# A long-convolution and feed-forward kernel: six of eight product groups copied whole out of PSUM, GpSimd's time counted in full by the planner, and one PSUM buffer for two quarters of the inverse

## The chip, the cores and the metric

The kernel runs on one core of one Trainium2 chip. The metric is the device time of one execution in microseconds (us). Before the change the median of three runs is 644.57 us, from 643.6 to 645.45. One further execution was profiled: it took 642.35 us, of which 640.6 us lie between its first and last instruction (its span).

In the profile the engines are PE (matmuls), PEld (PE's weight loads, which overlap the matmuls), DVE (VectorE), ACT (ScalarE), POOL (GpSimd) and SP (SyncE, which here issues transfers).

## The reference

Two branches work on 2048 positions of 640 channels, and a gate per position mixes them.

```python
def _A_ref(u, log_A_real, A_imag, C_real, C_imag, log_dt, D_skip):
    ...
    P = jnp.exp((A * dt[:, None])[:, :, None] * pos[None, None, :])
    K = 2.0 * jnp.einsum("dn,dnl->dl", C, P).real
    ...
    y = jnp.fft.irfft(Uf * Kf[None, :, :], L2)[:, :, :L]
    return y + u * D_skip[None, None, :]

def _B_ref(x, w1, w2):
    h = jnp.maximum(jnp.einsum("bsd,df->bsf", x, w1), 0)
    return jnp.einsum("bsf,fd->bsd", h, w2)

g = _sigmoid((x * gate_w).sum(-1, keepdims=True))
return g * a + (1 - g) * b
```

Branch A builds one filter of 2048 taps for each channel from 128 complex modes and convolves the channel with it. Branch B is a two-layer network with 1728 hidden units. All arithmetic is in 32 bits.

## The kernel before

**The feed-forward branch** runs in three parts over the hidden units (`PARTS`), each over eight groups of 256 positions. Every matrix is split in a high and a low half, so that a product takes three matmuls. Its matmuls write the PSUM tile `pf` (two banks in turn); ACT and DVE take the hidden layer out of it (`hh`, `hl`), and DVE merges the sums of the second layer into `q`. These are the fillers: most have the lowest rank on PE.

**The generator** (up to about 404 us) makes the filter taps with sines and exponentials on ACT and multiplications on DVE, and POOL adds the skip term to a tile `kt`.

**The convolution** (`conv`, from about 404 us on) is a transform of 4096 points, done in five blocks of 128 channels (i = 0 to 4). One block goes through:

- *first step* (`stage1`): matmuls with a table `tf` on the filter (`ck`, `cl`) and on the input (`xu`), and DVE transposes into the large tile `ku`, which has two halves, K and U, for eight groups j;
- *second step* (`stage2`), for each group j: 32 small matmuls with the table `tm` write one PSUM buffer `pc`, whose two halves are the spectra of the filter and of the input. ACT copies the filter half to SBUF, over the group's K. DVE multiplies it by the imaginary part of the input, read from PSUM, into the group's U, and then by the real part, in place. POOL forms the complex product with a subtraction and an addition;
- *inverse of the second step* (`inv2`), for each half h of four groups: 128 matmuls with the table `tn` into two buffers `pc`, copied back by ACT;
- *relay*: eight DVE transposes from U to K;
- *last step* (`inv1`): for each j of two and each quarter q of two, matmuls with the table `tw` (two in the code, four rows in the profile) write one buffer `pc`, from which ACT takes four gated columns into `yo`. POOL joins parts of the feed-forward sum to these, and SP stores them.

The PSUM ring `psc` has three buffers `pc` of two banks each. All four steps take from it; `inv2` takes two at once. Another ring, `K`, has two tiles `ku`, so the next block's first step can run while this block is in its second.

**The order of all work** is written by a planner (`Plan`) before the program exists. Every piece of work is a task with an engine, an assumed duration, tasks it depends on, ring tokens that it takes and uses, and a rank (lower is sooner). `Plan.run` repeatedly picks the task that can start soonest and issues it; the engines then execute in exactly this order, each as a fixed queue, and wait where reality is later than the plan. A token goes back to its ring when its last user ends. A task with `port=True` lengthens DVE's assumed time when POOL is assumed busy; before the change only the generator's DVE tasks have this mark. On PE the plan prefers to stay with fillers (mode `f`) until two convolution tasks (`c`, `c1`) are ready or 3 us have passed, and it charges 0.2 us for a change of mode. SP's queue is part of the same order.

`stage2` puts its eight matmul tasks, then `inv2` for h = 0 and for h = 1, into one queue `s2`, so that they reach PE in this order. The multiplications have rank `S2D` = 1 on DVE, merges and hidden-layer corrections rank 0, relays rank 2.

Of the kernel before, what the change touches and what calls it, by code (L numbers as in the profile page):

```python
# [10 lines left out]
F32 = mybir.dt.float32  # L11
# [14 lines left out]
S4R = 3  # L26
# [27 lines left out]
S2D = 1  # L54
# [5 lines left out]
PL = 2.5  # L60
YO = 5
YJ = 3
KRANK = 3
TN = 0.7

# [76 lines left out]
class Plan:  # L142
# [79 lines left out]
    def run(self):  # L222
        self.free = {e: 0.0 for e in self.LAG}
        mode, dma, log, done, block, since = {}, 0.0, [], 50.0, 0.0, 0.0
        heads = {k: 0 for k in self.queues}
        while True:
            best = None
            for e in self.LAG:
                c, soon = [], []
                for (eng, q), n in heads.items():  # L230
                    if eng == e and n < len(self.queues[eng, q]):
                        t = self.queues[eng, q][n]
                        r, known = self.ready(t)
                        for g in t.glue:
                            r2, k2 = self.ready(g)
                            r, known = max(r, r2), known and k2
                            for b in t.take:
                                k = sum(x.ring is b.ring for x in (*t.take, *g.take))
                                r = max(r, sorted(b.ring.slots)[k - 1] if len(b.ring.slots) >= k else 1e9)
                        (c if known else soon).append((r, t))  # L240
                if not c:
                    continue
                at = max(self.free[e], min(r for r, _ in c))
                key = lambda t: t.prio + (0.5 if t.mode is not None and mode.get(e) not in (None, t.mode) else 0)
                r, t = min((x for x in c if x[0] <= at), key=lambda x: key(x[1]))
                start = max(at, r)
                if e == 'PE' and mode.get(e) == 'f':


                    if t.mode in self.BURST and at - since < self.PATIENCE and self.burst(c, heads, at) < self.GATHER:  # L250
                        other = [x for x in c if x[1].mode == 'f' and x[0] <= at + .05]
                        if other:
                            r, t = min(other, key=lambda x: key(x[1]))
                            start = max(at, r)
                if e == 'PE' and (t.mode != 'f' or mode.get(e) != 'f'):

                    for r2, t2 in c:
                        if key(t2) < key(t) and r2 <= at + self.HOLD:
                            t, start = t2, max(at, r2)
                    hold = [r2 for r2, t2 in soon if t2.prio < t.prio and r2 <= at + self.HOLD]  # L260
                    if hold:
                        at = max(hold)
                if best is None or at < best[0]:
                    best = at, e, t, start
            if best is None:
                break
            _, e, t, start = best
            change = self.CHANGE.get(e, 0) if t.mode is not None and mode.get(e) not in (None, t.mode) else 0
            if e == 'PE' and t.mode != 'f':
                since = start + t.dur  # L270
            if t.mode is not None:
                mode[e] = t.mode
            for b in t.take:
                b.ring.slots.remove(min(b.ring.slots))
            t.fn()
            self.free[e] = start + change + t.dur
            if e == 'PE':

                done += t.n
                while done >= 128:  # L280
                    done -= 128
                    at = self.free[e] - t.dur * done / t.n
                    fetch = self.FETCH + (self.BUSY if dma > at + 2 else 0)
                    self.free[e] += max(0, block + fetch - at)
                    block = max(at, block + fetch)
            if t.port:

                self.free[e] += 0.25 * min(max(self.free['POOL'] - start, 0), t.dur)
            t.end = self.free[e] + t.lag
            if t.kb:  # L290
                dma = max(dma, start + min(t.dur, 0.62) + 0.5) + t.kb / (230 if start < 12 else 270)
                t.end = max(dma, start + t.dur) + 1.1
            for b in (*t.take, *t.use):
                b.left -= 1
                b.free = max(b.free, t.end)
                if b.left == 0:
                    b.ring.slots.append(b.free)
            heads[e, t.q] += 1
            log.append((start, t))
        stuck = [(k, self.queues[k][n]) for k, n in heads.items() if n < len(self.queues[k])]  # L300
        assert not stuck, [(k, len(self.queues[k]) - heads[k]) for k, _ in stuck]
        self.log = log
# [42 lines left out]
class Kernel:  # L345
# [865 lines left out]
    def conv(self, C=128):  # L1211
        tc, nc, io, A, tok, ring = self.tc, self.nc, self.io, self.plan.add, self.plan.token, self.plan.ring
        V, S, P, D_ = self.V, self.S, self.P, self.D
        n, H = D // C, C // 2
        od = self.out.rearrange("(a h b) d -> h a b d", h=2, b=16)
        ud = io['A_u'][0].rearrange("(a b) d -> a b d", b=32)
        for k, v in dict(psc=3, ck=2, ckp=2, cu=1, yo=YO, yj=YJ, K=2).items():
            ring(k, v)
        st = {}

# [96 lines left out]
        def stage2(i, j, dep):  # L1317
            b_ = tok('psc')

            def pe():  # L1320
                ps = self.psc.tile([128, 2, 4, C], F32, name="pc")
                for a in range(2):
                    for m in range(4):
                        for p in range(2):
                            r, g = slice(p * 64, p * 64 + 64), 4 * j + m
                            x = st['ku', i].rearrange("p j k (e m t) -> p j m k e t", m=4, t=2)
                            self.E.matmul(ps[32 * m:32 * m + 32, p, 2 * a:2 * a + 2].rearrange("q k (e t) -> q k e t", t=2),
                                          st['tm'][r, g, 32 * a:32 * a + 32], x[r, j, m], start=True, stop=True)
                st['p2', i, j] = ps.rearrange("q p (a k) c -> q k a p c", a=2)

            def copy():
                S.copy(whole(i, j), st['p2', i, j][:, 0])

            def mul(a):
                def go():
                    k = whole(i, j)
                    V.tensor_mul(whole(i, j, 'U') if a else k, st['p2', i, j][:, 1, None, a].to_broadcast([128, 2, 2, C]), k)
                return go

            def add(k):  # L1340
                def go():
                    y, x = whole(i, j)[:, k], whole(i, j, 'U')[:, 1 - k]
                    (P.tensor_add if k else P.tensor_sub)(y, y, x)
                return go
            f = A('PE', None, 0.92, pe, dep, take=[b_], use=[K[i]], rank=S2P, mode='c', n=32)
            c = [A('ACT', 's2', 0.52, copy, [f], use=[b_, K[i]], rank=0.5)]
            for a in (1, 0):
                c.append(A('DVE', 's2', 0.62, mul(a), c, use=[b_, K[i]], rank=S2D))
            return f, [A('POOL', 's2', 0.7, add(k), c, use=[K[i]], rank=1) for k in range(2)]


        def whole(i, j, k='K'):
            return st[k, i][:, j].rearrange("q (b p c) -> q b p c", b=2, p=2)
# [40 lines left out]
        def inv1(i, j, dep):  # L1394
            last = i == n - 1
            for q in range(2):
                b_, b0 = tok('psc'), j * 8 + q * 4
                ns = min(max(2 * sum(c <= i for c in CG) - b0, 0), 4)
                y_ = tok('yo') if ns or not last else None
                g_, first = None, False  # L1400
# [1 line left out]
                    first = self.gy_tok is None  # L1402
                    g_ = self.gy_tok = self.gy_tok or tok('K')

                def pe(q=q, b0=b0):
                    py = st['p4', i, b0] = self.psc.tile([128, 2, 4, C], F32, name="pc")
                    for h in range(2):
                        self.E.matmul(py[h * 64:h * 64 + 64, 0].rearrange("p b c -> p (b c)"), st['tw'],
                                      st['K', i][:, h * 4 + b0 // 4], start=True, stop=True)

                def copy(q=q, b0=b0, ns=ns, y_=y_, first=first):
                    if first:
                        self.gy = self.pr.tile([128, 8, 2, 512], F32, name="ku", bufs=2).rearrange("p j k (b c) -> p (j k b) c", c=C)
                    if y_:
                        st['yo', i, b0] = self.pr.tile([128, 4, C], F32, name="yo", bufs=YO)
                    x = st['p4', i, b0][:, 0].rearrange("p b c -> p (b c)").rearrange("p (c b) -> p b c", b=4)
                    for b in range(4):
                        o = self.gy[:, b0 + b] if last and b >= ns else st['yo', i, b0][:, b]
                        S.mul(o, x[:, b], self.gate[:, b0 + b:b0 + b + 1])
                a = A('PE', 's4', 0.87, pe, [*dep, tw], take=[b_], use=[K[i]], rank=S4R, mode='c1')  # L1420
                pes['4', i, b0] = a
                if JS4 and q:
                    self.plan.join([pes['4', i, b0 - 4], a])
# [117 lines left out]
```

## Time and profile before

| | |
|---|---|
| median of three runs | 644.57 us (643.6 to 645.45) |
| profiled execution | 642.35 us, span 640.6 us |
| granted PE clock | 1.00 over the whole span |
| transfers | 107.78 MB, mean 168 GB/s |
| ACT busy from 404 to 641 us | 82 us of 237 |
| POOL busy from 404 to 641 us | 83 us of 237 |

In the profile's rows a group of instructions is named by the tile it writes and the tiles it reads, `out<-in`; nearly all carry line 314, the helper that pins each instruction in the planner's order. "Idle before" is time in which the engine did nothing ahead of the group, with what ended that wait. In the view by stretches each row is a stretch of the span with the busy time and number of instructions of each engine. In the view in order of time, rows of the same kind that follow each other are merged, with their count.

### The profile page before, as it was taken

The page shows a single profiled execution, that of the slowest core. Times are in us where ns is not written, and L with a number is a line of the kernel's source. Part 1 is how long each engine was busy: PE and PEld are TensorE (multiplying, and loading weights), DVE is VectorE, ACT ScalarE, POOL GpSimd, SP SyncE. Part 2 cuts the span into 40 slices and gives each one's busy share as a digit, 9 for nine tenths or more (in the row PEclk, how much of TensorE's full clock was granted, in tenths as well). Part 3 has the DMA queues.
Part 4 walks back from the last instruction along what each step waited for, and adds up shares of the span by engine and source line. Part 5 has one row for each costly group of instructions (what it writes and reads, how often), then busy time and mean ns, then how long its engine had stood idle before and what let it go on. Part 6 is the DMA issues. An engine that isn't in the chain of part 4 may idle for free.

```text
span 640.6 us, 19212 instructions
## 1 busy us (share of the span) xinstructions
PE 617.3 (96%) x8236; PEld 503.0 (79%) x8236; DVE 508.5 (79%) x818; ACT 402.1 (63%) x603; POOL 93.9 (15%) x134
## 2 busy tenths in 40 slices
PE   7989999899999899999999999999999999999897
PEld 6989998798898798898898898665565556756577
DVE  4889936989999999998999999768579753966542
ACT  5557439999999988988978985113443424432550
POOL 0000000000000000000000000024151531713633
PEclk9999999999999999999999999999999999999999
DMA  9974774333456734373454225794406558156355
GB/s 256 326 236 147 221 229 165 105 125 112 136 167 210 255 122 144 122 242 117 129 198 154 79 80 176 258 315 132 144 3 215 185 164 263 53 158 188 102 166 133
DMA packets 76176, 107.78 MB, mean 168 GB/s; under 512 B 7610, under 2 KB 58682, under 8 KB 75195
## 3 DMA queue, kind: packets, MB, share of 16 engines
q1 hardware_dynamic: 75930, 106.14, 53.2%
q8 instruction: 65, 1.06, 0.7%
q10 hardware_dynamic: 160, 0.41, 0.3%
q14 instruction: 21, 0.16, 0.1%
HBM read 67.47 MB, written 44.30 MB: 174 GB/s over the span
## 4 chain that ended last, share of the span: by engine, by line
PE 56%; DVE 5%; DMA 2%; ACT 2%; issue 1%; SPq 1%; DVEq 0%; ACTq 0%
PE pf L314 35%; PE pc L314 13%; PE pk L314 4%; DVE ku L314 3%; PE pg L314 2%; PE px L314 2%; DMA part<-q 1%; ACT ku L314 1%; PE pe L314 1%; DMA out_dram<-yo 1%; SPq L314 1%; DVE sn L314 1%; ACT cs L314 0%; DVE q L314 0%; ACT q L314 0%
## 5 line engine op out<-in xcount | busy, mean ns | idle before, releaser
L314 PE MATMUL pf<-xx,w1h 128*128 128x256 f32 (+1 forms) x760 | 184.2, 339 | 0.4 <-DVE xx L314 0.3
L314 PEld LDWEIGHTS pf<-xx,w1h 128*128 128x128 f32 x760 | 125.2, 189 | 22.8 <-issue 7.3
L314 PE MATMUL pf<-xx,w1l 128*128 128x512 f32 (+1 forms) x340 | 115.7, 340 | 0.0
L314 PE MATMUL pf<-w2h,hh 128*128 128x320 f32 x288 | 89.7, 315 | 2.4 <-DVE hl L314 1.5
L314 PE MATMUL pf<-w2l,hh 128*128 128x320 f32 x288 | 87.8, 309 | 0.0
L314 ACT COPY ku<-pc 128x512 f32<-128x512 f32 (+1 forms) x60 | 43.8, 761 | 68.2 <-PE pc L314 56.7
L314 PE MATMUL pf<-w2h,hl 128*128 128x320 f32 x256 | 73.3, 312 | 0.0
L314 PEld LDWEIGHTS pf<-xx,w1l 128*128 128x128 f32 x340 | 64.3, 189 | 7.6 <-DVE w1l L314 0.2
L314 POOL TENSOR_TENSOR kt<-kt,dsk 128x8 f32<-128x8 f32 x20 | 10.3, 515 | 392.7 <-DVE kt L314 377.8
L314 POOL TENSOR_TENSOR ku<-ku 128x256 f32<-128x256 f32 x80 | 56.2, 737 | 55.3 <-DVE ku L314 49.1
L314 DVE TENSOR_TENSOR ku<-pc,ku 128x512 f32<-128x512 f32 x80 | 52.6, 684 | 12.5 <-ACT ku L314 11.3
L314 DVE STREAM_TRANSPOSE ku<-pc 128x512 f32<-128x512 f32 x80 | 50.2, 683 | 13.7 <-PE pc L314 13.7
L314 PEld LDWEIGHTS pf<-w2h,hh 128*128 128x128 f32 x288 | 54.1, 188 | 7.7 <-issue 3.7
L314 DVE TENSOR_TENSOR sn<-pg,cs 128x1024 f32<-128x1024 f32 x40 | 48.7, 1217 | 7.5 <-ACT cs L314 7.5
L314 PEld LDWEIGHTS pf<-w2l,hh 128*128 128x128 f32 x288 | 54.1, 188 | 0.6
L314 ACT ACT_TABLE_LOAD x42 | 53.9, 1283 | 0.7
L314 ACT CAST cs<-pg 128x1024 int32<-128x1024 f32 x40 | 40.3, 1008 | 21.2 <-PE pg L314 21.0
L314 DVE TENSOR_TENSOR mg<-mg,cs 128x1024 f32<-128x1024 f32 x40 | 48.9, 1222 | 1.3
L314 PEld LDWEIGHTS pf<-w2h,hl 128*128 128x128 f32 x256 | 46.4, 188 | 3.5 <-issue 2.9
L314 PE MATMUL pc<-ku,tm 64*32 64x256 f32 x1280 | 42.2, 392 | 3.6 <-DVE ku L314 2.4
L314 ACT ACTIVATE cs<-cs,half_pi 128x1024 f32<-128x1024 f32 x40 | 45.6, 1140 | 0.0
L314 ACT ACTIVATE hh<-pf 128x512 fp32r<-128x512 f32 (+1 forms) x40 | 20.5, 513 | 39.4 <-PE pf L314 39.4
(170 smaller groups left out, 1232.5 us busy)
## 6 DMA issues: line engine op xcount, KB each, us to landing
xx<-xt SPq DMA_DIRECT2D x24, 640.0 KB, 6.8
xt<-xx SPq DMA_DIRECT2D x16, 640.0 KB, 3.9
part<-q SPq DMA_DIRECT2D x16, 640.0 KB, 3.4
q<-part SPq DMA_DIRECT2D x16, 640.0 KB, 5.3
ws<-in_B_w_dram SPq DMA_DIRECT2D x20, 320.0 KB, 5.5
kd<-kt SPq DMA_DIRECT2D x80, 64.0 KB, 1.8
ub<-in_A_u_dram SPq DMA_DIRECT2D x10, 512.0 KB, 4.7
xu<-ub SPq DMA_DIRECT2D x5, 1024.0 KB, 6.2
```

What stands on the lines that cost most here:

```text
L314: self._last = self._tc.keep_in_program_order(f(*a, **k))
```

## The change

In `stage2`, for the groups j = 0, 1, 2, 4, 5 and 6 of every block (`FULL`), ACT copies all 1024 columns of the buffer into the group's K and U (before: 512 columns into K). Both multiplications of DVE then read the input's spectrum from U in SBUF in place of PSUM, and the first writes a new SBUF tile `ut` of a ring of two in place of U. They no longer use the PSUM token, so the buffer is free after the copy. POOL's two additions read `ut` and give it back. Groups 3 and 7 stay as they were. The plan's duration of the copy is 0.96 in place of 0.52 for full groups, and their multiplications are marked `port`.

In `Plan.run` the share of POOL's remaining time that is charged to a `port` task goes from a quarter to the whole.

In `inv1` the two quarters of one j write the two halves of one buffer `pc`: the second quarter takes no token of its own, and the buffer is free when both are copied.

```diff
+FULL = (0, 1, 2, 4, 5, 6)
+UT = 2
+FULLR = 0
...
-                self.free[e] += 0.25 * min(max(self.free['POOL'] - start, 0), t.dur)
+                self.free[e] += 1.0 * min(max(self.free['POOL'] - start, 0), t.dur)
...
-        for k, v in dict(psc=3, ck=2, ckp=2, cu=1, yo=YO, yj=YJ, K=2).items():
+        for k, v in dict(psc=3, ck=2, ckp=2, cu=1, yo=YO, yj=YJ, K=2, ut=UT).items():
...
+            full = j in FULL
+            t_ = tok('ut') if full else None
+
             def copy():
-                S.copy(whole(i, j), st['p2', i, j][:, 0])
+                if full:
+                    S.copy(st['ku', i][:, j].rearrange("q k (a p c) -> q k a p c", a=2, p=2), st['p2', i, j])
+                else:
+                    S.copy(whole(i, j), st['p2', i, j][:, 0])
...
                     k = whole(i, j)
-                    V.tensor_mul(whole(i, j, 'U') if a else k, st['p2', i, j][:, 1, None, a].to_broadcast([128, 2, 2, C]), k)
+                    u = whole(i, j, 'U')[:, a] if full else st['p2', i, j][:, 1, a]
+                    if a:
+                        st['x2', i, j] = whole(i, j, 'U')
+                        if full:
+                            st['x2', i, j] = self.pr.tile([128, 4 * C], F32, name="ut", bufs=UT).rearrange("q (b p c) -> q b p c", b=2, p=2)
+                    V.tensor_mul(st['x2', i, j] if a else k, u[:, None].to_broadcast([128, 2, 2, C]), k)
...
-                    y, x = whole(i, j)[:, k], whole(i, j, 'U')[:, 1 - k]
+                    y, x = whole(i, j)[:, k], st['x2', i, j][:, 1 - k]
...
-            c = [A('ACT', 's2', 0.52, copy, [f], use=[b_, K[i]], rank=0.5)]
+            c = [A('ACT', 's2', 0.96 if full else 0.52, copy, [f], use=[b_, K[i]], rank=0.5)]
             for a in (1, 0):
-                c.append(A('DVE', 's2', 0.62, mul(a), c, use=[b_, K[i]], rank=S2D))
-            return f, [A('POOL', 's2', 0.7, add(k), c, use=[K[i]], rank=1) for k in range(2)]
+                c.append(A('DVE', 's2', 0.62, mul(a), c, take=[t_] if full and a else (), use=[K[i]] + ([] if full else [b_]), rank=S2D + FULLR * full,
+                           port=full))
+            return f, [A('POOL', 's2', 0.7, add(k), c, use=[K[i]] + ([t_] if full else []), rank=1) for k in range(2)]
...
-                b_, b0 = tok('psc'), j * 8 + q * 4
+                b0 = j * 8 + q * 4
+                b_ = b_ if q else tok('psc')
...
-                    py = st['p4', i, b0] = self.psc.tile([128, 2, 4, C], F32, name="pc")
+                    if not q:
+                        st['p4', i, j] = self.psc.tile([128, 2, 4, C], F32, name="pc")
+                    py = st['p4', i, j]
...
-                        self.E.matmul(py[h * 64:h * 64 + 64, 0].rearrange("p b c -> p (b c)"), st['tw'],
+                        self.E.matmul(py[h * 64:h * 64 + 64, q].rearrange("p b c -> p (b c)"), st['tw'],
...
-                a = A('PE', 's4', 0.87, pe, [*dep, tw], take=[b_], use=[K[i]], rank=S4R, mode='c1')
+                a = A('PE', 's4', 0.87, pe, [*dep, tw], take=() if q else [b_], use=[K[i]] + ([b_] if q else []), rank=S4R, mode='c1')
```

More of the change, by code (lines that the diff above doesn't have):

```diff
@@ L1403, in inv1, with pe, copy @@
                     g_ = self.gy_tok = self.gy_tok or tok('K')
-                def pe(q=q, b0=b0):
-                    py = st['p4', i, b0] = self.psc.tile([128, 2, 4, C], F32, name="pc")
+                def pe(q=q, b0=b0, j=j):
+                    if not q:
+                        st['p4', i, j] = self.psc.tile([128, 2, 4, C], F32, name="pc")
+                    py = st['p4', i, j]
                     for h in range(2):
-                        self.E.matmul(py[h * 64:h * 64 + 64, 0].rearrange("p b c -> p (b c)"), st['tw'],
+                        self.E.matmul(py[h * 64:h * 64 + 64, q].rearrange("p b c -> p (b c)"), st['tw'],
                                       st['K', i][:, h * 4 + b0 // 4], start=True, stop=True)
-                def copy(q=q, b0=b0, ns=ns, y_=y_, first=first):
+                def copy(q=q, b0=b0, ns=ns, y_=y_, first=first, j=j):
                     if first:
```

2 lines of the change are left out of this document (1 added, 1 removed).

## The prediction

> **What bounds the kernel now.** I read the engine table of the page first, then the busy time by stretches, the list of waits from 404 us on, and the chain that ended last.
>
> ```profile
> span 640.6 us, 19212 instructions
> PE 617.3 (96%) x8236; PEld 503.0 (79%) x8236; DVE 508.5 (79%) x818; ACT 402.1 (63%) x603; POOL 93.9 (15%) x134
> ```
> ```profile
> core 0: us, PE busy (x) PEld busy (x) DVE busy (x) ACT busy (x) POOL busy (x), PEclk, DMA share, GB/s
> 404.00:641.00 237.00, 227.84 (x3540) 147.66 (x3539) 151.05 (x247) 81.95 (x166) 82.98 (x108) 1.00 0.54 164
> 499.00:516.00 17.00, 16.69 (x305) 10.27 (x302) 12.59 (x20) 6.77 (x16) 11.70 (x17) 1.00 0.51 151
> 583.00:603.00 20.00, 17.40 (x304) 11.13 (x302) 11.77 (x19) 9.79 (x25) 14.37 (x19) 1.00 0.49 136
> ```
> PE is the bound: 227.84 of the 237 us in which the convolution runs, at full clock. The last two rows are the second step of the third and the fifth block of channels; only the fifth leaves PE visibly idle. DVE has 86 us of air in the stage, but in a second step it has only 4 of 17.
>
> ```profile
> POOL ku L314 <- DVE ku L314: 49.1, 11, 24.1
> PE pc L314 <- DVE ku L314: 3.1, 6, 1.7
> PE pc L314 <- ACT ku L314: 1.0, 1, 1.0
> ```
> PE waits in the open for 4.1 us on account of the second step's buffers. The rest of what they cost is hidden in changes between feed-forward matmuls (pf) and convolution matmuls (pc). Five stretches of PE alone show these: three groups with free buffers, the feed-forward filler after them, three groups that met full buffers, two groups with free buffers; then filler and two groups of the fifth block.
>
> ```profile
> core 0: us, PE busy (x), PEclk, DMA share, GB/s
> 425.06:427.98 2.92, 2.92 (x98) 1.00 1.05 299
> 427.98:428.91 0.93, 0.93 (x13) 1.00 1.01 240
> 428.91:432.27 3.36, 3.19 (x97) 1.00 0.56 190
> 434.22:436.23 2.01, 2.01 (x66) 1.00 0.70 201
> 591.00:594.72 3.72, 2.03 (x20) 1.00 0.92 235
> 594.72:597.70 2.98, 2.31 (x65) 1.00 0.31 86
> ```
> Counts include instructions cut by an edge. Three groups take 2.92, two take 2.01, so one is 0.91 and entering the mode costs 0.19. The filler of 0.93 us is five matmuls of 320 columns; the tail of the chain gives their pace.
>
> ```profile
> 623.67 13.12 PE pf L314 x88
> 636.81 0.02 DVEq L314
> 636.88 0.55 DVE q L314
> ```
> 13.12 / 88 = 0.149, so five are 0.745 and going back costs 0.19 too. A there-and-back is worth 0.38 us. These rows also give the end: PE stops at 636.8 and 3.8 us of merging and storing follow. As 13 us of feed-forward work stand behind the last convolution matmul, the convolution's own latency does not set the end; PE's total does.
>
> **The change part by part.**
>
> *The copies.* In six of eight groups ACT takes both halves out of PSUM, and the buffer comes free before DVE starts.
>
> ```profile
> L314 DVE TENSOR_TENSOR ku<-pc,ku 128x512 f32<-128x512 f32 x80 | 52.6, 684 | 12.5 <-ACT ku L314 11.3
> L314 ACT COPY ku<-pc 128x512 f32<-128x512 f32 x40 | 23.3, 593 | 42.7 <-PE pc L314 42.7
> L314 ACT COPY ku<-pc 128x1024 f32<-128x1024 f32 x20 | 20.7, 1095 | 25.5 <-PE pc L314 14.0 <-issue 11.5
> L314 DVE TENSOR_TENSOR G<-mg,sn 128x512 f32<-128x512 f32 x40 | 27.4, 685 | 0.0
> L314 POOL TENSOR_TENSOR ku<-ku 128x256 f32<-128x256 f32 x80 | 56.2, 737 | 55.3 <-DVE ku L314 49.1 <-PE pf L314 6.2
> ```
> ACT pays 30 x (1.095 - 0.593) = 15 us, beside 82 busy of 237: hidden under PE. Without that cover it is at most 0.5 us for each filler activation queued behind a longer copy. The multiplication itself costs the same from SBUF (685, the row of the generator) as from PSUM (684): nothing won on DVE. Hold time of a buffer behind the matmul falls from 0.593 + 2 x 0.684 = 1.96 to 1.10 us, near PE's 0.91 per group, so three buffers nearly let PE run through. There are 11 filler stretches inside the five second steps (two or three in each, the first at 427.98 and the last at 591.00). All gone is 11 x 0.38 = 4.2 us, none gone is 0. I take 8, because groups 3 and 7 still hold theirs until DVE arrives: **-3.0**. Of the 4.1 us of open waits I take two thirds, **-2.7**; the wait after 591.00 is partly ACT's own lateness and stays (bounds 0 and -4.1).
>
> *The lock between DVE and POOL.* The multiplications now read two SBUF operands while POOL adds from SBUF. The only such meeting before is a tiny POOL add in the generator.
>
> ```profile
> 121.04 0.21 POOL L314 TENSOR_TENSOR kt<-kt,dsk 128x8 f32<-128x8 f32 x1 [119.61 <-DVE kt L314]
> 159.12 0.57 POOL L314 TENSOR_TENSOR kt<-kt,dsk 128x8 f32<-128x8 f32 x1 [19.88 <-DVE kt L314]
> ```
> ```profile
> 158.97 0.65 DVE L314 SCALAR_TENSOR_TENSOR G<-mg,sn 128x512 f32<-128x512 f32 x1
> 159.54 0.69 DVE L314 TENSOR_TENSOR G<-mg,sn 128x512 f32<-128x512 f32 x1
> ```
> Alone it takes 0.21; begun inside a DVE operation with two SBUF inputs it takes 0.57 and ends at 159.69, 0.07 after that operation. POOL waits, then, and the next DVE operation at 0.69 lost almost nothing to an add of eight columns. No row has a long add in DVE's way. Lower bound 0. Upper bound one whole add, 0.70 at POOL's pace, for each multiplication that follows a group still being added: two each in groups 1, 2, 4, 5 and 6, so 10 x 0.70 = 7.0 us per block of DVE lag. The feed-forward filler forgives some of it: it has two banks of its own, and a sum of 12 matmuls gives 12 x 0.149 = 1.8 us of grace. Of DVE's 17 us in the third block's step 12.59 are busy. I take one add per block reaching PE, 5 x 0.70 = **+3.5**, near the lower end, as filler and other DVE work between multiplications let POOL finish.
>
> [...]
>
> *The spare buffers.* The first multiplication of a full group waits for one of two product buffers, freed by POOL. Queued behind it on DVE are merges and hidden-layer corrections, for which PE waits. Cover: two groups of distance; without it, one POOL pair, 2 x 0.737 = 1.5 us. I put it inside the lock's term.
>
> *Quarter pairs.* Two quarters of the last step now take one buffer.
>
> ```profile
> 478.47:481.68 3.21, 3.07 (x16) 1.00 0.00 0
> 511.23:513.63 2.40, 2.09 (x12) 1.00 0.85 198
> 597.70:600.03 2.33, 2.09 (x9) 1.00 0.00 0
> 620.01:623.60 3.59, 3.58 (x17) 1.00 0.38 107
> ```
> Sixteen unhindered matmuls take 3.59, 0.90 for four. Twelve at 478.47 take 3.21 instead of 2.70, eight at 597.70 take 2.33 instead of 1.80: 0.5 us at each of four such places, the first at 478.47 and the last at 597.70. Half of 2.0 goes: **-1.0** (bounds 0, -2.0). It also leaves two buffers where there was one:
>
> ```profile
> 507.18 8.36 POOL L314 TENSOR_TENSOR ku<-ku 128x256 f32<-128x256 f32 x12 [0.21 <-DVE ku L314]
> ...
> 519.67 1.15 ACT L314 ACTIVATE yo<-pc,gate 128x128 f32<-128x128 f32 x4 [1.73 <-PE pf L314]
> 522.53 1.14 ACT L314 ACTIVATE yo<-pc,gate 128x128 f32<-128x128 f32 x4 [1.72 <-DMA y__84<-yo]
> 531.64 0.58 PE L314 MATMUL pc<-ku,tn 32*64 32x128 f32 x24
> ```
> Two quarters issued at 511.23 held a buffer each until these two ACT rows. The adds were done at 515.5, but the inverse step, which takes two buffers of three, came at 531.64. One holder fewer lets it start up to 16 us sooner. I cost that at 0: PE was busy with filler meanwhile, and 13 us of it are left at the end.
>
> *The planner's factor.* It executes nothing; it moves instructions on every queue, SP's transfers with them, though no DMA is added. The generator's multiplications are charged too, beside 20 POOL adds of 0.21 to 0.57 us. Value 0; bounds 2 us to either side, five there-and-backs of PE at 0.38 more or fewer.
>
> **Sum:** -3.0 - 2.7 - 1.0 + 3.5 = -3.2 us on the span, 640.6 to 637.4. The profiled execution's time is 642.35, 1.8 over its span, and so 639.2 after; it lies 2.2 under the median of the runs, 644.57, which gives **641.4**.
>
> **The rivals.**
>
> *The lock decides (slower).* Place: DVE's queue in the second step. The plan charges DVE only for adds already placed when a multiplication is placed; I work that out as about 1.3 us per block of the 7.0, and POOL's own waits as none. The order on PE is fixed, so filler waits for late merges and the inverse step for late adds. Lag beyond plan and grace is 7.0 - 1.3 - 1.8 = 3.9 per block, 19.5 in all; with the gains of 6.7 it is +12.8, about 657; half of it, where gaps in DVE's queue absorb some, is +3, 648. It decides from 6.7 / 5 = 1.3 us per block reaching PE. For it: in the fifth block the chain that ended last runs through DVE's multiplications, and POOL's adds stand there without a pause.
>
> ```profile
> 596.86 1.30 DVE ku L314 x2
> ```
> ```profile
> 591.28 11.11 POOL L314 TENSOR_TENSOR ku<-ku 128x256 f32<-128x256 f32 x16
> ```
> Against: DVE's 86 us of air in the stage.
>
> *More than I take.* All fillers and waits go and the lock hides: -4.2 - 4.1 - 2.0 = -10.3, 634. Against: groups 3 and 7 hold buffers, and inverse and transposing matmuls want the same three.
>
> *Nothing moves.* PE still changes modes as often, because the plan prefers short filler, and buffers fall free only to wait for POOL: gains of 3.5 eaten by 3.5 of lock, 644.5. For it: POOL's 49.1 us of waiting for DVE say the adds are paced by multiplications that get no shorter.
>
> **How the numbers follow.** A run of this kernel tells about 0.3%, 1.9 us, from no change: faster means below 642.6, slower above 646.5. Forecast (636 to 642.6): 0.37. More than I take: 0.10. Nothing moves: 0.11. The lock: 0.32, most of it between 647 and 655. A worse order from the moved factor and copies, +3 to +8 us: 0.10. So faster 0.47, same 0.11, slower 0.42. The range 632 to 655 takes the best case, with 2 us for the order, and the lock up to nine tenths of its 19.5; the forecast's own is 636 to 642.6.
>
> **What would show it.** Copies of 1024 columns rise from 20 to 50 and the second step's matmuls stand in one or two runs per block: right on the buffers. Multiplications from SBUF near 685 with POOL adds near 737: the lock is cheap; either well over 0.9 us shows its price. PE rows waiting for DVE or POOL (ku, or pf behind a merge) beyond 4.1 us mean the rival. The forecast is wrong if PE's fillers inside the second step stay at ten or so, or if PE's idle time from 404 us on passes 9 us.

## The result, and the profile after

The changed kernel takes 654.13 us, median of seven runs (652.68 to 659.39); the kernel before takes 643.52 in the same comparison (642.06 to 645.45). The ratio is 1.0177, 95% interval 1.0155 to 1.0199: **slower by 1.8%**, where 641.4 was forecast. Executions in which the chip granted a clearly lower clock (one of e14's four below: 756.05 us at a mean of 0.752) are left out of all ratios. The profiled execution is the slowest of the seven, 659.39 us with a span of 657.5.

The engine table of the page of the kernel after:

```profile
span 657.5 us, 19208 instructions
PE 623.5 (95%) x8236; PEld 511.1 (78%) x8236; DVE 523.2 (80%) x818; ACT 412.4 (63%) x603; POOL 109.5 (17%) x134
```

The span grew by 657.5 - 640.6 = 16.9 us. PE is 623.5 - 617.3 = 6.2 us busier with the same 8236 matmuls, and idle for 10.7 us more. DVE is busy for 14.7 us longer and POOL for 15.6, with as many instructions as before. The groups of the convolution, shapes kept apart, say which:

```profile
L317 POOL TENSOR_TENSOR ku<-ku,ut 128x256 f32<-128x256 f32 x60 | 53.8, 923 | 64.8 <-DVE ku L317 41.8 <-ACT ku L317 23.0
L317 ACT COPY ku<-pc 128x1024 f32<-128x1024 f32 x50 | 49.9, 1058 | 60.3 <-PE pc L317 60.2
L317 DVE TENSOR_TENSOR ku<-ku 128x512 f32<-128x512 f32 x30 | 28.4, 946 | 2.3
L317 DVE TENSOR_TENSOR ut<-ku 128x512 f32<-128x512 f32 x30 | 27.9, 929 | 11.9 <-ACT ku L317 7.0 <-issue 3.0 <-POOL ku L317 1.9
L317 POOL TENSOR_TENSOR ku<-ku 128x256 f32<-128x256 f32 x20 | 18.6, 948 | 0.9 <-DVE ku L317 0.9
L317 DVE TENSOR_TENSOR ku<-pc,ku 128x512 f32<-128x512 f32 x20 | 13.7, 683 | 0.3
```

The twenty multiplications that still read PSUM take 683 ns, as before. The sixty that read two SBUF operands take 929 and 946, and POOL's additions 923 and 948 in place of 737. DVE loses 30 x (0.929 - 0.684) + 30 x (0.946 - 0.684) = 15.2 us. The copies of 1024 columns are there, 50 of them, at 1058 ns (the twenty of before: 1095).

What PE waits for from 404 us on (total, times, longest):

```profile
PE pc L317 <- DVE ku L317: 9.9, 8, 3.6
PE pf L317 <- ACT w2h L317: 2.3, 1, 2.3
PE pf L317 <- DVE q L317: 2.3, 2, 1.4
PE pc L317 <- ACT yo L317: 0.7, 2, 0.3
```

Before, the first of these was 3.1 us. The longest wait of the 9.9 ends at 477.11. These are the rows in order of time that lead to it (start, duration; rows of the same kind that follow each other are merged):

```profile
471.07 4.01 POOL L317 TENSOR_TENSOR ku<-ku,ut 128x256 f32<-128x256 f32 x4 [22.31 <-ACT ku L317]
471.63 1.04 DVE L317 TENSOR_TENSOR ku<-ku 128x512 f32<-128x512 f32 x1
...
472.60 0.70 DVE L317 STREAM_TRANSPOSE ku<-ku 128x512 f32<-128x512 f32 x1
...
473.31 1.20 DVE L317 TENSOR_TENSOR ut<-ku 128x512 f32<-128x512 f32 x1
474.61 1.02 DVE L317 TENSOR_TENSOR ku<-ku 128x512 f32<-128x512 f32 x1
475.56 1.40 DVE L317 TENSOR_TENSOR ku<-pc,ku 128x512 f32<-128x512 f32 x2
475.78 1.41 POOL L317 TENSOR_TENSOR ku<-ku,ut 128x256 f32<-128x256 f32 x2 [0.69 <-DVE ku L317]
...
477.11 0.68 PE L317 MATMUL pc<-ku,tm 64*32 64x256 f32 x8 [3.58 <-DVE ku L317]
```

Here the whole mechanism can be seen. While POOL adds, a multiplication from SBUF takes 1.02 to 1.20 us and each of POOL's four additions 1.00, against means of 0.68 and 0.74 in the kernel before: each engine holds up the other. The transposition at 472.60, with one SBUF operand, takes 0.70 amid the same additions (the forty of its form take 681 ns on average). As soon as DVE multiplies from PSUM (475.56, two in 1.40), POOL's two additions take 1.41 too, 0.70 each. Those two from PSUM belong to group 3, which still holds its buffer until DVE has read it; they stand in DVE's queue behind the slow ones, and PE starts 0.15 us after they end. The waits that end at 438.41, 524.11 and 606.10 (1.33, 1.54 and 2.08 us) also end just after such a pair.

PE's 6.2 us of extra busy time are its clock. Stretches of the same profile (busy time of PE, PEld, DVE, ACT, POOL; granted clock; DMA share; GB/s):

```profile
471.00:474.40 3.40, 2.53 (x63) 1.27 (x43) 3.28 (x4) 2.42 (x3) 3.33 (x4) 1.00 0.00 0
474.40:478.00 3.60, 0.89 (x21) 0.56 (x29) 3.35 (x6) 0.00 (x0) 2.91 (x4) 0.75 0.00 0
478.00:481.00 3.00, 3.00 (x57) 1.47 (x42) 2.90 (x3) 1.15 (x2) 3.00 (x4) 0.50 0.02 5
481.00:484.00 3.00, 3.00 (x10) 2.34 (x10) 0.14 (x1) 0.45 (x1) 2.10 (x3) 0.67 0.00 0
```

From about 476.2, still in the gap, until 483.0 the granted clock of PE is 0.50. Half clock comes with the gaps that end at 606.10 and 638.75 too, for 3.4 us each (0.50 from about 605.9 to 609.3 and from 640.0 to 643.4). Together these are some 13.6 us at half clock, so about 6.8 us of work put off, near the 6.2 that PE is busier; an estimate. The mean clock of this execution is 0.984; of the median run 0.992, of runs of the kernel before about 0.998. At 0.992 some (0.998 - 0.992) x 654 = 4 of the 11 us would be clock and the rest direct waiting, an estimate.

### The profile page after: what moved, and what is told of

Same layout as the page of the kernel before. It is cut to its first block, busy times and chain, and to the rows that moved or that the text cites. A ratio compares the mean times of both kernels' runs of the same rounds, so it can differ in the third digit from the quotient of the medians.

```text
span 657.5 us, 19208 instructions
## 1 busy us (share of the span) xinstructions
PE 623.5 (95%) x8236; PEld 511.1 (78%) x8236; DVE 523.2 (80%) x818; ACT 412.4 (63%) x603; POOL 109.5 (17%) x134
## 4 chain that ended last, share of the span: by engine, by line
PE 69%; DVE 15%; ACT 5%; DMA 5%; issue 3%; SPq 2%; POOL 1%; DVEq 0%; POOLq 0%; ACTq 0%
PE pf L317 47%; PE pc L317 10%; PE pk L317 6%; DVE ku L317 4%; DVE ut L317 3%; PE pg L317 2%; PE px L317 2%; SPq L317 2%; DVE sn L317 1%; DMA xu<-in_A_u_dram 1%; PE pe L317 1%; ACT yo L317 1%; DVE G L317 1%; POOL ku L317 1%; DMA part<-q 1%
## 5 line engine op out<-in xcount | busy, mean ns | idle before, releaser
L317 ACT COPY ku<-pc 128x1024 f32<-128x1024 f32 (+1 forms) x60 | 54.9, 983 | 61.5 <-PE pc L317 61.5
L317 POOL TENSOR_TENSOR ku<-ku,ut 128x256 f32<-128x256 f32 x60 | 53.8, 923 | 64.8 <-DVE ku L317 41.8
L317 ACT ACTIVATE hh<-pf 128x512 fp32r<-128x512 f32 (+1 forms) x40 | 20.5, 512 | 49.5 <-PE pf L317 49.5
L317 PE MATMUL pc<-ku,tm 64*32 64x256 f32 x1280 | 44.2, 413 | 6.8 <-DVE ku L317 6.1
L317 PEld LDWEIGHTS pc<-ku,tm 64*32 64x32 f32 x1280 | 24.4, 110 | 24.8 <-issue 8.3
```

What stands on the lines that cost most here:

```text
L317: self._last = self._tc.keep_in_program_order(f(*a, **k))
```

## The experiments

Two names serve below: the **lock** is the mutual lengthening of DVE's multiplications from SBUF and POOL's additions; **DVE's lateness** is what PE sees of it. Every kernel is a variant of the kernel after, so that a part left out leaves the rest as it is. Ratios are to the kernel before on the same chip.

### The parts by themselves

e1 keeps the copies alone, e2 the quarter pairs alone, e3 the factor alone.

```diff
# against the kernel after; e1 and e2:
-                self.free[e] += 1.0 * min(max(self.free['POOL'] - start, 0), t.dur)
+                self.free[e] += 0.25 * min(max(self.free['POOL'] - start, 0), t.dur)
# e2 and e3:
-FULL = (0, 1, 2, 4, 5, 6)
+FULL = ()
# e1 and e3 (tile, matmul and copy go back with it):
-                b0 = j * 8 + q * 4
-                b_ = b_ if q else tok('psc')
+                b_, b0 = tok('psc'), j * 8 + q * 4
...
```

> Only the whole copies (six of eight groups) with their product buffers; factor a quarter as before, one buffer for each quarter as before. Lock theory (DVE's products and POOL's adds exclude each other in the second step, and PE's fixed order waits): slower than before by 8 us or more, 651 to 660, with products from SBUF above 0.9 us and POOL's adds above 0.9 us on average; with the factor at a quarter the plan knows of less waiting, so not better than the changed kernel. Order theory (the moved factor and the pairs spoil the order of the work, the copies cost nothing): 642 to 647, the products still near 0.69 us or their lengthening without waits on PE.

> Only the shared buffer of the quarter pairs. Lock theory: 641 to 645, no lengthened products, PE's open waits for the second step's buffers near the 4.1 us of before. Order theory, if the pairs are at fault: 648 or more, with the gate copies of the last step standing in front of a feed-forward copy on ACT near the end.

> Only the planner's factor, 1.0 in place of 0.25, on the generator's DVE work. Lock theory: 642 to 645, as nothing executed changes and 20 small adds are all it counts. Order theory, if the factor is at fault: 648 or more, lost before 411 us.

e1: 658.06 us, 1.0226 (1.0193 to 1.026), multiplications at 978 and 984, additions at 938 and 928, PE behind DVE's ku 10.7 us, as the lock theory had it. e2: 645.39 us, 1.0039 (1.0021 to 1.0057), between the two ranges. e3: 641.4 us, 0.997 (0.9953 to 0.9988), a little below its range. The copies alone bring the whole loss; the factor gains 1.9 us, and the pairs, forecast at -1.0, cost 2.5 us. The waits of PE in e2 have a row that the kernel before has not got, the second of these:

```profile
PE pc L317 <- DVE ku L317: 2.8, 3, 2.4
PE pc L317 <- ACT yo L317: 2.4, 4, 0.8
```

PE waits for ACT's gated copies: a pair holds its buffer until both quarters are copied. That these 2.4 us are the 2.5 is likely and not tested by itself.

e15 has factor and pairs without copies, e12 copies and factor without pairs.

```diff
# e15
-FULL = (0, 1, 2, 4, 5, 6)
+FULL = ()
# e12
-                b0 = j * 8 + q * 4
-                b_ = b_ if q else tok('psc')
+                b_, b0 = tok('psc'), j * 8 + q * 4
...
```

> Factor and quarter pairs without any whole copy: what the copies are to be measured against. If the two add as they do alone (-1.7 and +2.3 us): 643 to 645, so that the copies without their lock (641.6) were worth 2 to 3 us and with it cost 10. If 640 or less, the copies are worth nothing even without the lock.

> The changed kernel without the shared buffer of the quarter pairs: whole copies and the factor. If factor and pairs add to the copies as they do alone (-1.7 and +2.3 us): 651 to 654, so that the factor does the little that parts this from the copies alone. If only the pairs help the copies: 656 to 660.

e15: 647.67 us, 1.0058 (1.0029 to 1.0086), above its forecast, so factor and pairs, -1.9 and +2.5 us apart, make +3.7 together. Its trace has a wait of PE near the end that neither e2 nor e3 has:

```profile
PE pf L317 <- ACT w2h L317: 2.8, 1, 2.8
```

ACT takes `w2h` from 625.71 on there, straight behind all the gated copies of the last step; in e2 it does so before them (620.08), in e3 before the last four (621.31). These 2.8 us are near what factor and pairs cost beyond their sum. e12: 661.06 us, 1.0258 (1.0182 to 1.0334), above the kernel after, so that with copies the pairs help if anything; the intervals overlap. Whether the pairs gain or cost depends on the order they fall into.

### Is it the lock?

e4 leaves everything else in its place and lets POOL add 8 of 256 columns; e5 does so in the kernel before, as a control; e6 lets POOL write zeros and read nothing. In all three the order of the program is the same as without the edit.

```diff
# e4, e5
+                    y, x = y[:, :, :4], x[:, :, :4]
                     (P.tensor_add if k else P.tensor_sub)(y, y, x)
# e6
-                    (P.tensor_add if k else P.tensor_sub)(y, y, x)
+                    P.memset(y, 0.0)
```

> The changed kernel in its own order, but POOL's adds of the second step work on 8 of 256 columns, so most of the complex product is left out. Lock theory: products from SBUF fall to about 0.69 us, PE's waits for them to under 5 us from 404 us on, and the time to 638 to 645. Order theory: the time stays above 650, as the order is the same.

> Control for the cut: the kernel before, in its own order, with POOL's adds of the second step on 8 of 256 columns, so most of the complex product is left out. Lock theory: before has no such lock, the cut takes only POOL's pace away, 639 to 644. If the cut gains here what it gained in the changed kernel (about 11 us, to 632), then it was POOL's time and not the lock.

> The changed kernel in its own order, POOL's adds of the second step replaced by filling the same 256 columns with zeros: POOL writes SBUF and reads none, the complex product is left out. Lock theory, by POOL's reads: products from SBUF at 0.66 to 0.72 us, time 640 to 647. If POOL's writes or its time on the path are at fault: products above 0.85 us or the time above 650.

e4: 643.21 us, 0.9981 (0.9959 to 1.0003). e5: 642.12 us, 0.9978 (0.9958 to 0.9999): without copies, faster additions are worth about 1.4 us (0.1 to 2.6). e6: 641.59 us, 0.9986 (0.9962 to 1.0011). All three lie where the lock theory put them. The groups of e6:

```profile
L317 POOL MEMSET ku<- 128x256 f32 x80 | 22.7, 313 | 94.5 <-DVE ku L317 64.9 <-ACT ku L317 27.0 <-ACT q L317 1.9
L317 DVE TENSOR_TENSOR ku<-ku 128x512 f32<-128x512 f32 x30 | 21.6, 720 | 2.3
L317 DVE TENSOR_TENSOR ut<-ku 128x512 f32<-128x512 f32 x30 | 20.3, 677 | 10.0 <-ACT ku L317 7.0 <-issue 3.0
```

With nothing read by POOL the multiplications are back at 677 and 720. The lock is worth (1.0177 - 0.9986) x 643.5 = 12.3 us, some 2 us either way by the two intervals, and no less than the whole loss. Beside e15, the copies without their lock gain (1.0058 - 0.9986) x 643.5 = 4.6 us. What PE waits for in e6:

```profile
PE pc L317 <- DVE ku L317: 3.5, 3, 2.3
PE pf L317 <- ACT w2h L317: 1.7, 1, 1.7
PE pc L317 <- issue: 1.5, 2, 0.9
PE pc L317 <- ACT yo L317: 0.3, 1, 0.3
```

### Whose lateness counts?

The lock makes both engines late, and e6 takes away both delays. e13 gives POOL its delay back without a lock (three fills for each addition); e10 gives DVE some of its loss (a fill of 256 columns, 272 ns, behind each multiplication of a full group), e17 a larger one (384 columns, 378 ns), and e14 gives both. All four leave out the complex product, as e6 does.

```diff
# e13, e14 (e10 and e17 have e6's single fill)
-                    (P.tensor_add if k else P.tensor_sub)(y, y, x)
+                    for _ in range(3):
+                        P.memset(y, 0.0)
# e10 (256), e17 and e14 (384)
+        self.scr = keep.tile([128, 384], F32, name="scr")
...
                     V.tensor_mul(st['x2', i, j] if a else k, u[:, None].to_broadcast([128, 2, 2, C]), k)
+                    if full:
+                        V.memset(self.scr, 0.0)
```

> The changed kernel's order without the lock, POOL filling each target three times with zeros, some 0.94 us in place of each add (under the lock an add took 0.92 on average), the complex product left out. If the lock costs through POOL's late adds: 648 to 656. If POOL's side costs nothing by itself: 641 to 644.

> The changed kernel's order without the lock (POOL fills zeros in place of the adds), and after each product from SBUF one more DVE instruction that fills 256 scratch columns, unknown to the planner, 60 of some 0.2 to 0.3 us: DVE loses about as much as the lock took (some 15 us), POOL nothing. If the lock costs through DVE's lateness: 649 to 656, with PE waiting for products again. If it costs through POOL's late adds: 641 to 645.

> Both sides of the lock's lost time without the lock: POOL fills each target three times, DVE fills 384 scratch columns after each product from SBUF (60 of some 0.3 us). If the lock is no more than time lost on both engines: 650 to 656, near the changed kernel. If it stays at 643 to 648, the lock costs by where it strikes (the products of groups 1, 2, 5 and 6 alone, back to back), and not by its sum.

> The second step's copies as changed, GpSimd's adds of the complex product replaced by fills of zeros (0.31 us each, one each), and VectorE given 60 more fills of 384 columns (378 ns each in e14). It is e14 without GpSimd's threefold fills. If VectorE's lost time alone makes PE wait: as e14, 649 to 655, PE behind VectorE's ku 7 to 9 us. If it takes the lateness of both engines: 643 to 647, as e10 (644.86 with 272 ns each), PE behind VectorE's ku about 6.

All have the same order, so they can be set side by side; e17 ran on another chip than e6, e13, e10 and e14, and its ratio is to the kernel before on that chip. Busy times are those from 404 us on:

| | DVE busy | POOL busy | ratio |
|---|---|---|---|
| e6, fills | 152.5 | 49.5 | 0.9986 (0.9962 to 1.0011) |
| e13, POOL three times | 152.5 | 97.2 | 0.9978 (0.9951 to 1.0005) |
| e10, DVE +9.5 | 162.1 | 49.8 | 1.0024 (0.9993 to 1.0054) |
| e17, DVE +15.6 | 168.1 | 49.6 | 1.0167 (1.0124 to 1.021) |
| e14, DVE +16.1, POOL three times | 168.7 | 98.1 | 1.0119 (1.0068 to 1.017) |
| after, with the lock | 167.3 | 98.6 | 1.0177 (1.0155 to 1.0199) |

The rows behind two of them, stretches of the kernel after and of e17, and the groups of e17 that show DVE's fills and its multiplications free of the lock:

```profile
404.00:665.00 261.00, 234.10 (x3670) 154.90 (x3668) 167.28 (x249) 93.65 (x168) 98.61 (x108) 0.97 0.50 151
```
```profile
404.00:665.00 261.00, 230.48 (x3651) 152.28 (x3640) 168.13 (x307) 92.41 (x167) 49.59 (x108) 0.98 0.50 149
```
```profile
L317 DVE MEMSET scr<- 128x384 f32 x60 | 22.7, 378 | 1.8
L317 DVE TENSOR_TENSOR ut<-ku 128x512 f32<-128x512 f32 x30 | 20.3, 677 | 10.0 <-ACT ku L317 7.0 <-issue 3.0
L317 DVE TENSOR_TENSOR ku<-ku 128x512 f32<-128x512 f32 x30 | 19.1, 636 | 0.0
```

POOL's lateness by itself costs nothing that shows: e13 (641.87 us) is as fast as e6. e10 (644.86 us) lies in the range that its forecast gave to POOL's late additions, and it could not tell, as its DVE lost 9.5 us in place of some 15. DVE's lateness alone, in e17 (653.24 us), gives the time of the kernel after without any lock, and PE's waits come back with it, 6.8 us behind DVE's ku and 3.0 behind its merges:

```profile
PE pc L317 <- DVE ku L317: 6.8, 8, 2.6
PE pf L317 <- DVE q L317: 3.0, 3, 1.5
```

**The loss is DVE's lost time.** e14, with POOL late on top, is no slower than e17. The loss is not proportional: the first 9.5 us cost 0.4% (2.4 us, which the two intervals do not tell from nothing), the next 6.1 cost 1.4% (9.2 us). So there is some slack, and past it more is lost than DVE is late. Part of that is the clock: 0.995 to 0.996 in the median of e10's runs, 0.990 in that of e17's, some 3 to 4 us of 650, an estimate.

### Three attempts to keep the copies

e7 tells the planner the price of the lock (0.92 us for each multiplication of a full group and each addition); e11 is e7's order with fills in place of additions. e8 gives the additions of full groups to DVE, so that little meets. e9 makes all eight groups full, so that none holds its buffer until DVE has read it. In e7, e8 and e9 the planner writes a new order.

```diff
# e7, e11
-                c.append(A('DVE', 's2', 0.62, mul(a), c, ..., port=full))
-            return f, [A('POOL', 's2', 0.7, add(k), c, ...
+                c.append(A('DVE', 's2', 0.92 if full else 0.62, mul(a), c, ..., port=False))
+            return f, [A('POOL', 's2', 0.92, add(k), c, ...
# e8
-                    (P.tensor_add if k else P.tensor_sub)(y, y, x)
+                    e = V if full else P
+                    (e.tensor_add if k else e.tensor_sub)(y, y, x)
-            return f, [A('POOL', 's2', 0.7, add(k), c, ...
+            return f, [A('DVE' if full else 'POOL', 's2', 0.36 if full else 0.7, add(k), c, ...
# e9
-FULL = (0, 1, 2, 4, 5, 6)
+FULL = (0, 1, 2, 3, 4, 5, 6, 7)
```

> The changed kernel with a planner that knows the lock: 0.92 us for each product from SBUF and for each add of the second step, nothing charged by the factor there. Undercount theory (the loss is the fixed order, made for times that do not hold): 642 to 648, PE's open waits for the products from 404 us on back to 4 us or less. Capacity theory (DVE and POOL together are too slow for the convolution whatever the order): 650 to 657.

> The order of the planner that knows the lock, with POOL filling zeros in place of the adds, so without the lock. If that order lost 19 us to the lock after all: 641 to 648. If the order itself is worse: 652 or more, with the waits that it had.

> The changed kernel with the adds of the six full groups on DVE in place of POOL, planned at 0.36 us each: no lock in those groups, 60 more DVE instructions of about 0.42 us. Lock theory: products from SBUF below 0.75 us, time 643 to 649. If DVE's load alone is at fault: 650 or more, as DVE carries 0.8 us more for each full group against about 0.5 us of lock.

> The changed kernel with all eight groups copied whole. If PE waits in the second step because groups 3 and 7 hold their buffers until DVE reaches them late, PE's open waits for the products fall from 9.9 us to 3 or less and the time to 646 to 651, though 20 more products and adds exclude each other. If PE pays for DVE's lost time as such, wherever it is lost, the time rises to 655 to 662.

e7: 662.37 us, 1.029 (1.0247 to 1.0334), above both of its ranges; e11: 653.55 us, 1.0141 (1.0083 to 1.0199). This plan, which knows the durations, is no cure: its order is itself worse than that of e6 by (1.0141 - 0.9986) x 643.5 = 10 us, and the lock adds as much again. What in that order is worse stays open.

e8: 663.92 us, 1.0336 (1.0285 to 1.0387). The multiplications are nearly free of the lock (681 and 730; the twenty additions left to POOL take 883), but sixty additions of 428 ns make DVE busier than the lock did:

```profile
404.00:665.00 261.00, 233.47 (x3539) 152.75 (x3537) 174.24 (x306) 92.47 (x165) 43.72 (x48) 0.97 0.49 149
```

e9: 658.47 us, 1.0216 (1.0164 to 1.0268), as forecast if DVE's lost time counts wherever it is lost. With all buffers free PE hardly waits for products any more (1.5 us), but for the merges behind them:

```profile
PE pf L317 <- DVE q L317: 13.3, 8, 3.6
PE pc L317 <- issue: 3.0, 3, 1.3
PE pc L317 <- DVE ku L317: 1.5, 5, 0.5
```

So the buffers of groups 3 and 7 are one place where DVE's lateness came out; with those gone, in an order of its own, it comes out in the filler's banks.

### Fewer copies

e16 copies only group 0 whole, e18 groups 0 and 4; both keep the factor and leave out the pairs.

```diff
# e16: (0,); e18: (0, 4)
-FULL = (0, 1, 2, 4, 5, 6)
+FULL = (0,)
-                b0 = j * 8 + q * 4
-                b_ = b_ if q else tok('psc')
+                b_, b0 = tok('psc'), j * 8 + q * 4
...
```

> Factor at 1.0, no pairs, and only group 0 of each block copied whole: its products run before POOL has an add of the block, so they meet no lock. Products from SBUF at 0.68 to 0.75 us. If whole copies are worth something where no lock strikes: 638 to 641, below the factor alone (641.4). If not: 641 to 645.

> The moved factor, no shared quarter pairs, and whole copies for groups 0 and 4 only, two of eight. If what counts is how much VectorE and GpSimd meet, and the first group of each half meets little: 637 to 640, at or below e16's 639.39, products from SBUF under 850 ns. If every further whole copy costs by its lock: 641 to 646, products over 850 ns, PE behind VectorE's ku over 4 us.

e16: 639.39 us, 0.994 (0.9916 to 0.9965), **faster than both kernels**, than the one before by 0.6%. Of its ten multiplications from SBUF the five first ones take 848 ns on average and the five second ones 692. The 848 come from one that took 1.49 us; the other four took 0.65 to 0.75. So the lock is all but gone. PE's waits behind DVE's ku are 0.9 us, against 3.1 before and 1.2 in e3, the factor alone. The groups, the one long multiplication with POOL's addition beside it, and the waits:

```profile
L317 DVE TENSOR_TENSOR ut<-ku 128x512 f32<-128x512 f32 x5 | 4.2, 848 | 8.8 <-ACT ku L317 5.7 <-issue 3.0
L317 DVE TENSOR_TENSOR ku<-ku 128x512 f32<-128x512 f32 x5 | 3.5, 692 | 0.5
```
```profile
508.72 1.29 POOL L317 TENSOR_TENSOR yo<-yo,yj 128x512 f32<-128x512 f32 x1 [0.16 <-DMA yj<-part]
509.07 1.49 DVE L317 TENSOR_TENSOR ut<-ku 128x512 f32<-128x512 f32 x1 [2.78 <-ACT ku L317]
```
```profile
PE pc L317 <- DVE ku L317: 0.9, 2, 0.6
PE pc L317 <- issue: 0.5, 1, 0.5
```

This addition belongs to the output and not to the complex product, so not only the additions of the second step meet the multiplications.

Its interval overlaps that of the factor alone (e3), so that a share of the one copy in this gain is not shown. e18: 641.73 us, 0.998 (0.995 to 1.0011): neither theory as written, since PE waits only 0.6 us for DVE's ku and yet nothing that shows is gained over the kernel before. Its groups show the lock back on part of the multiplications; among the 946 one of group 0 took 1.80 us, again beside an addition of 1.29 for the output, and those of group 4 took 0.68 to 1.20:

```profile
L317 DVE TENSOR_TENSOR ut<-ku 128x512 f32<-128x512 f32 x10 | 9.5, 946 | 9.7 <-ACT ku L317 6.6 <-issue 3.0
L317 DVE TENSOR_TENSOR ku<-ku 128x512 f32<-128x512 f32 x10 | 8.0, 797 | 1.0
```

## Why the prediction was wrong

The direction was wrong; the time lies in the range, at its upper end, where the rival "The lock decides" put it (648 to 657). The rival had the mechanism, and its number by some luck: it took 7.0 us of lag per block, of which 3.9 or half of it would reach PE beyond plan and grace. The lag was 3.0, most of it arrived, and gains of 6.7 that it set against this did not come.

**The step that failed: "I take one add per block reaching PE, 5 x 0.70 = +3.5".** Measured between e6 and the kernel after, the term is 12.3 us. The lag itself was 15.2 / 5 = 3.0 us per block, between the bounds of 0 and 7.0. The slack that the prediction counted on is there (e10 loses 9.5 us on DVE and 2.4 in time), but past it PE waits (9.9 us behind DVE's ku, for 3.1 before) and runs at a clock of 0.50 for a while (some 13.6 us in all in the profiled execution), a cost that the prediction has no term for. The reason given, that "filler and other DVE work between multiplications let POOL finish", does not hold in the trace: from 471.07 to 475.08 POOL adds for two groups without a pause, and beside it DVE has multiplications of the groups behind with only a transposition between. A better guide was DVE's 12.59 busy of 17 us in the third block's step than its 86 us of air in the whole stage: sixty long operations that grow by a third fall into just such stretches, and the queue behind them is read by PE twice, through the buffers of groups 3 and 7 and through the filler's merges.

Beside additions that read SBUF the multiplications take 929 and 946 ns, beside e6's fills, which read nothing, 677 and 720. The prediction had no row with a long addition in DVE's way, so that the upper bound of 7.0 us per block, one whole addition for each multiplication, was the author's estimate and no run shows it. The lag measured was 3.0. The bound was too high, though with it the rival's sum came out on the right side.

**Round trips of PE, -3.0: half right.** Counted in order of time, filler stretches inside the five second steps fall from 11 to 6, both in the kernel after (at 434.09, 466.91, 472.56, 519.07, 558.16 and 603.02) and in e6: 5 x 0.38 = 1.9 us, an estimate, not 8 x 0.38. Beside e15 the copies without lock gain 4.6 us of the 5.7 forecast for both their terms; what the rest of the 4.6 is, the runs do not show.

**Open waits, -2.7: wrong.** In e6 PE still waits 3.5 us for DVE's ku, against 3.1 before, though nothing is locked. The prediction saw that groups 3 and 7 keep their buffers and took it off the round trips alone; 3.1 of the 3.5 us (2.26 and 0.80) stand ahead of group 6, right after DVE's pair from PSUM for group 3. It also did not see the tail: PE waits 1.7 us there for ACT's `w2h` (2.3 after), whose copy now stands behind the last step's gated copies; before, it came at 618.76 with PE still supplied. As e15 has this wait too, it is not the copies' doing.

**Quarter pairs, -1.0: wrong in sign alone (+2.5 in e2), and not additive.** The prediction counted the buffer that two quarters save, and not that a pair holds it for twice as many copies of ACT.

**The factor, 0 within 2: right in size**, -1.9 by itself. **The copies on ACT, hidden: right.** In the kernel after, PE's waits have no row for ACT's copies of the second step; before, there was one of 1.0 us. **The spare buffers, inside the lock's term: small**, since DVE waits 1.9 us in all for POOL ahead of the first multiplications. **The multiplication's own price, 685 from SBUF as from PSUM: right**, 677 and 720 in e6.

Without the lock the terms were forecast at -6.7 us; e6 has -0.9 (-2.4 to +0.7). So both sides of the sum were off: the gains by 5.8, the lock by 8.8. Of the 5.8, by far the most is pairs and factor together (-1.0 forecast, +3.7 in e15) and 1.1 the copies. Either error alone would have turned the sign: -6.7 + 12.3 and -0.9 + 3.5 are both above nothing.

Still open: what the half clock costs apart from the waits that precede it; why pairs and factor together put `w2h` so late on ACT; why the order of e7 is worse; why a second whole copy in e18 brings nothing.

## What to carry to other kernels

Before an operand is moved from PSUM to SBUF, look at which other engine reads SBUF while the reader works: here the buffers came free earlier as meant, and the reader became a third slower (929 and 946 ns for 684). Price such a slowdown at the stretch in which the slowed engine has no air, not by its idle time over a stage, and take it as reaching the engine that bounds the time in full once the slack of that stretch is used (here the first 9.5 us on DVE cost 2.4, the next 6.1 cost 9.2). To find out which of two delayed engines counts, give each its delay back by itself, with harmless work of the same length and in the same order.

## What the runs showed of the hardware

In e16 a multiplication of DVE with two SBUF operands that began within a long addition of POOL outlasted it: the addition ends at 508.72 + 1.29 = 510.01, the multiplication 0.55 us later, after 1.49 us (four others took 0.65 to 0.75 in all), while POOL's 1.29 is the average of the eight additions of this form (1292 ns). In e18 one took 1.80 us beside an addition of 1.29. In the kernel after, where both have work in their queues (471.07 to 475.08), neither stands still: of operations of 0.68 and 0.74 us in the kernel before, DVE's take 1.02 to 1.20 and POOL's 1.00. That is less than the 1.42 of both one after the other, so whole instructions by turns are not shown there.

The half clock of PE is not tied to a gap alone. In e14 PE has gaps of 2.59 and 2.26 us in the second and fifth block's step, the first of them one group of products later than in the kernel after, yet the granted clock is 1.00 through them:

```profile
470.00:475.00 5.00, 3.33 (x83) 1.61 (x67) 4.88 (x11) 3.14 (x4) 4.09 (x14) 1.00 0.01 3
475.00:480.00 5.00, 4.08 (x53) 2.92 (x61) 4.57 (x10) 1.18 (x2) 4.38 (x15) 1.00 0.00 0
600.00:604.00 4.00, 2.22 (x65) 1.56 (x66) 3.91 (x8) 2.13 (x4) 3.54 (x13) 1.00 0.02 4
```

In the kernel after, the gaps of 3.58 and 2.08 us in these steps came with half clock (0.50 for some 6.8 and 3.4 us), those of 1.33 and 1.54 did not (1.00 from 434 to 442 and from 520 to 528). e14 leaves out the complex product, so the data that PE reads differ as well. What decides whether a gap brings half clock, no run here shows.
